# Sink values stacked four times in 32 rows, and the values products in another order

## The chip, the cores and the metric

The kernel runs on one core of a Trainium2 chip. Times are microseconds of device time of that core. The engines go by the names of the profile: PE is TensorE (PEld its weight loads), DVE is VectorE, ACT is ScalarE, POOL is GpSimd, and SP is SyncE, which here issues nearly all DMAs.

## The reference

Two stages. First attention over q, k, v of shape (4 batches, 8 heads, 768 positions, 64): a query sees the keys of its window (the last 128 positions) and the first `n_sink` = 4 positions of its batch, the sinks.

```
scores = q @ k.T / sqrt(64)
keep = (pos < n_sink) | ((rel >= 0) & (rel < window))
a = softmax(where(keep, scores, -1e9))
out = a @ v
```

Then a dense part on the result, its heads side by side, as x of shape 3072 x 512:

```
h = x @ w_in          # 512 -> 2048
g = h * cos(h)
result = g @ w_out    # 2048 -> 512
```

## The kernel before

A head's six blocks of 128 queries are taken two at a time, 256 queries. Per batch the first pair of blocks forms an early chunk, the other two pairs form late chunks; the 32 early heads and 64 late heads are each one head of one such chunk. Late heads are the ones that the change touches. For one, TensorE makes the scores of each block (`scores`, L1024, 264 columns: 128 keys of the block, 8 sink columns padded from 4, 128 keys before it), VectorE masks and reduces them (L1046), ScalarE takes the exponential (L1055), a scaling by the row's denominator follows (L1075 where it is on VectorE), and TensorE turns the probabilities (`turn`, L1136) so that keys stand in partitions. To keep the precision of fp32 on fast products, a number is split into a rounded high part and the rest, the low part. Of the turned probabilities ScalarE writes the high part (L1162), VectorE the low one (L1167), and GpSimd cuts each into the two triangles of the window (`split`, L1174), into the tile `ph`. In the same way `vr` holds v's high and low parts side by side, 2 x 64 columns.

The values product of a late head (`values`, L1196 to 1219) then adds seven matmuls into one PSUM tile `av` of 128 x 256. A product with 128 weight columns multiplies by both parts of v, into rows 0 to 63 and 64 to 127; one with 64 weight columns by the high part alone. Three key blocks take part: the middle one serves both query blocks (256 moving columns), the outer ones one each (128). The two halves of `av` are added afterwards (L1222, L1234).

The sinks come in by a product of their own. `load_batch_v` (L852) loads the sinks' rows of v of a batch into `yt`, 8 DMAs. `vs_part` (L1091), one step for each of four slots of 32 partitions, writes their high and low parts into `x1r`, two VectorE operations on 16 rows a step. Per four heads, `sink_cols` (L1101) copies the sink columns of the probabilities into `gc` as high and low columns, 4 heads x 32 columns; `sink_turn` turns them (L1120), and `sink_out` copies the result to `gt`. The sinks' product multiplies `gt` (moving) by `x1r` (weights).

The dense part is two products of 512 moving columns: `h` (L476) and `acc` (L521), each of three parts (high by high, high by low, low by high), with the cosine between them on ScalarE and VectorE (L485 to L512). A planner (`Plan.order`, L70) sets the program order of each engine ahead of time from costs and due times in a table `C`, and engines run their own lists strictly in that order. Buffers are few: a load or a product waits until the last user of its buffer is through. In the opening, 0 to 64 us, where early heads run and weights arrive, TensorE's list is filled with products that nothing reads (L1532).

Names in the order rows below: `av_1_2_0` is the PSUM tile of a late head, `ph` and `vr` its probabilities and values, `gt` the turned sinks, `x1r` the sinks' values, `acc` the dense output.

Of the kernel before, what the change touches and what calls it, by code (L numbers as in the profile page):

```python
# [9 lines left out]
F32 = mybir.dt.float32  # L10
# [6 lines left out]
P = 128  # L17
NSINK = 8
SW = P + NSINK
GR = 96 + 2 * NSINK  # L20
BW = 2 * P + NSINK
INV2PI = 1.0 / (2.0 * math.pi)
TWOPI_DOWN = 6.283185
# [149 lines left out]
def attn_moe_kernel(ctx, tc, q, k, v, n_sink, window, w_in, w_out, out):  # L173
# [51 lines left out]
    neg, quarter = neg3[:, 0:2], neg3[:, 2:3]  # L225
# [7 lines left out]
    def setup():  # L233

        nc.scalar.dma_start(out=nw_i[:, 0, :], in_=n_sink.unsqueeze(0))
        nc.scalar.dma_start(out=nw_i[:, 1, :], in_=window.unsqueeze(0))
        nc.gpsimd.memset(ident, 0.0)
        nc.gpsimd.affine_select(
            out=ident, in_=ident, pattern=[[-1, P]], compare_op=ALU.not_equal, fill=1.0, base=0, channel_multiplier=1
        )  # L240

        nc.gpsimd.iota(rc_i[:, 0], pattern=[[-1, P]], base=0, channel_multiplier=1)
        nc.gpsimd.iota(rc_i[:, 1], pattern=[[1, P]], base=0, channel_multiplier=0)
        nc.vector.memset(ones, 1.0)
        nc.vector.memset(quarter, HALF_PI_DOWN)
        for raw, src in env.first:
            nc.scalar.dma_start(out=raw.rearrange("p n w -> p (n w)"), in_=src)
        nc.scalar.activation(out=tiny[:, 0:1], in_=quarter, func=AF.Exp)
        nc.vector.memset(f32(one_r), 1.0)
        nc.vector.tensor_copy(out=one_r, in_=f32(one_r))  # L250
        nc.vector.memset(lims, 0.0)
        nc.vector.memset(lims[:, 0, 1, 0:1], 1.0)
        nc.vector.memset(lims[:, 1, 0, 0:1], float(NSINK))
        nc.vector.memset(lims[:, 1, 1, 0:1], float(P))
        nc.vector.tensor_single_scalar(out=minus, in_=ident, scalar=-1.0, op=ALU.mult)
        nc.vector.tensor_copy(out=rc, in_=rc_i)
        nc.vector.tensor_single_scalar(out=env.below, in_=rel, scalar=0.0, op=ALU.is_lt)

        with tc.tile_pool(name="warm", bufs=1, space=PSUM) as pool:
            warm = pool.tile([P, P], F32, name="warm")  # L260
            both = pool.tile([P, 2], F32, name="both")
            for _ in range(C["WARM"]):
                nc.tensor.matmul(out=warm, lhsT=ident, rhs=ident, start=True, stop=True)

            nc.vector.tensor_copy(out=nw4, in_=nw_i)
            nc.tensor.matmul(out=both, lhsT=ones, rhs=nw4[:, :, 0], start=True, stop=True)
            for _ in range(C["WARM2"]):
                nc.tensor.matmul(out=warm, lhsT=ident, rhs=ident, start=True, stop=True)
            nc.vector.tensor_copy(out=neg, in_=both)
# [526 lines left out]
    def banded_path(ctx2):  # L796
# [33 lines left out]
        def x1r():  # L830

            if env.x1r is None:
                env.x1r = ap.tile([P, NP * NT], F32R, name="x1r", tag="x1")
                env.vs = env.x1r.rearrange("p (a b c d) -> p a b c d", a=NP, b=2, c=2)
            return env.x1r

        def sink_values():
# [14 lines left out]
        def load_batch_v(o):  # L852
            def fn(e):
                o.vs32 = xb[:, : 2 * D].rearrange("p (n d) -> p n d", d=D)
                for h in range(4):
                    for dup in range(2):
                        r0 = h * 32 + dup * 8
                        nc.sync.dma_start(
                            out=o.vs32[r0 : r0 + 8], in_=v[o.b, h::4, 0:NSINK, :].rearrange("p s d -> s p d")
                        )  # L860
            return fn
# [228 lines left out]

        def vs_part(o, h):  # L1091
            def fn(e):
                w = sink_values().rearrange("p (g a) b c d -> p g (a b) c d", g=2)
                r = slice(h * 32, h * 32 + 2 * NSINK)
                e.tensor_copy(out=w[r, :, h, 0, :], in_=o.vs32[r])
                e.tensor_tensor(
                    out=w[r, :, h, 1, :], in0=o.vs32[r], in1=f32(w)[r, :, h, 0, :], op=ALU.subtract
                )
            return fn

        def sink_cols(o, four):  # L1101
            def fn(e):
                j0 = o.sj[0]
                for h, oo in enumerate(four):
                    nc.vector.tensor_copy(out=gc.bitcast(F32R)[:, j0:, h * 32 : h * 32 + NSINK], in_=oo.p[:, j0:, P:SW])
                for h, oo in enumerate(four):
                    nc.vector.tensor_tensor(
                        out=gc[:, j0:, h * 32 + NSINK : h * 32 + 2 * NSINK], in0=oo.p[:, j0:, P:SW],
                        in1=gc[:, j0:, h * 32 : h * 32 + NSINK], op=ALU.subtract,
                    )  # L1110
            return fn

# [2 lines left out]

        def sink_turn(o):
            def fn(e):
                o.gp = late_bank(o, 2)[:GR]
                for n, j in enumerate(o.sj):
                    nc.tensor.transpose(  # L1120
                        out=o.gp[:, n * P : (n + 1) * P], in_=gc[:, j], identity=ident,
                    )
            return fn

        def sink_out(o):
            def fn(e):
                w = len(o.sj) * P
                copy(e, gt[:GR, :w], o.gp[:, :w])
            return fn

        def turn(o):
# [64 lines left out]
        def values(o):  # L1196


            def fn(e):
                o.av = late_bank(o, 1)  # L1200
                mms = {}
                for t, w in ((o.phi, 2 * D), (o.plo, D)):
                    for n, (kb, qs) in enumerate(o.cols):
                        dst = o.av[:w, (qs[0] - o.i0) * P : (qs[-1] + 1 - o.i0) * P]
                        lhs = o.vr[:, kb - o.kb0].rearrange("p a d -> p (a d)")[:, :w]
                        mms.setdefault((w, len(qs)), []).append((dst, lhs, t[:, o.offs[n] * P : o.offs[n + 1] * P]))
                (wide_hi,), (wide_lo,) = mms[2 * D, CB], mms[D, CB]
                narrow = [m for pair in zip(mms[2 * D, 1], mms[D, 1]) for m in pair]
# [485 lines left out]
        gc = ap.tile([P, CB, GR], F32, name="gc")  # L1694
        env.x1f = ap.tile([P, NP, PT], F32, name="x1f", tag="x1")

        for _, _, fn, e in steps:
# [155 lines left out]
```

## Time and profile before

| what | value |
|---|---|
| median of 3 runs | 726.91 us (726.79 to 726.95) |
| span of the profiled execution | 725.6 us |
| PE busy | 708.8 us (98%) |
| PEld busy | 584.1 us (81%) |
| DVE busy | 599.3 us (83%) |
| ACT busy | 527.7 us (73%) |
| POOL busy | 127.5 us (18%) |

The profiled execution is listed by its span, from the first to the last instruction; a run's time also holds what lies around that. Busy times of PE overlap the engine's own pipelining, so a busy PE is not one at its peak. Four stages can be told apart: the opening to 64 us, early heads with dense products to 182, late heads with dense products to 620, dense products alone to the end. Within the third, batches begin near 185, 293, 405 and 517 us with the split of their sinks' values.

### The profile page before, as it was taken

The page shows a single profiled execution, that of the slowest core. Times are in us where ns is not written, and L with a number is a line of the kernel's source. Part 1 is how long each engine was busy: PE and PEld are TensorE (multiplying, and loading weights), DVE is VectorE, ACT ScalarE, POOL GpSimd, SP SyncE. Part 2 cuts the span into 40 slices and gives each one's busy share as a digit, 9 for nine tenths or more (in the row PEclk, how much of TensorE's full clock was granted, in tenths as well). Part 3 has the DMA queues.
Part 4 walks back from the last instruction along what each step waited for, and adds up shares of the span by engine and source line. Part 5 has one row for each costly group of instructions (what it writes and reads, how often), then busy time and mean ns, then how long its engine had stood idle before and what let it go on. Part 6 is the DMA issues. An engine that isn't in the chain of part 4 may idle for free.

```text
span 725.6 us, 12986 instructions
## 1 busy us (share of the span) xinstructions
PE 708.8 (98%) x3674; PEld 584.1 (81%) x3674; DVE 599.3 (83%) x1849; ACT 527.7 (73%) x1344; POOL 127.5 (18%) x213
## 2 busy tenths in 40 slices
PE   7998999999999999999999999999999999999996
PEld 7766787888888888888888888888888888888884
DVE  6889998988988978988978988878989865667762
ACT  3896976788697697796686886776887766566642
POOL 1010000001223222232231222232123222100000
PEclk9999999999999999999999999999999999999999
DMA  5665555533256333355433254433254500375551
GB/s 144 182 186 153 158 162 162 141 65 68 68 118 146 73 62 57 72 119 124 93 60 59 56 131 103 118 61 64 43 139 99 119 18 12 97 210 148 164 137 64
DMA packets 236501, 77.13 MB, mean 106 GB/s; under 512 B 221060, under 2 KB 221060, under 8 KB 236420
## 3 DMA queue, kind: packets, MB, share of 16 engines
q1 hardware_dynamic: 236128, 75.15, 43.4%
q10 hardware_dynamic: 292, 1.05, 0.5%
q8 instruction: 32, 0.52, 0.3%
q14 instruction: 49, 0.40, 0.2%
HBM read 69.86 MB, written 6.29 MB: 105 GB/s over the span
## 4 chain that ended last, share of the span: by engine, by line
PE 81%; ACT 11%; DVE 4%; issue 2%; DMA 1%; SPq 0%; ACTq 0%; DVEq 0%
PE acc L521 32%; PE h L476 32%; PE av L1215 5%; PE s L1024 4%; ACT p L1055 3%; PE s L968 2%; PE av L1191 2%; PE tp L1136 2%; ACT p L1073 1%; PE tp L1146 1%; PE qk L931 1%; ACT L485 1%; PE idle L1532 1%; ACT L1055 1%; ACT early L390 1%
## 5 line engine op out<-in xcount | busy, mean ns | idle before, releaser
L521 PE MATMUL acc<-whi_out,ghi 128*128 128x512 f32 x384 | 161.8, 421 | 0.0
L476 PE MATMUL h<-xhi,whi_in 128*128 128x512 f32 x384 | 155.2, 404 | 0.0
L476 PE MATMUL h<-xlo,whi_in 128*128 128x512 f32 x384 | 150.9, 393 | 0.0
L521 PE MATMUL acc<-whi_out,glo 128*128 128x512 f32 x384 | 150.8, 393 | 0.0
L521 PE MATMUL acc<-wlo_out,ghi 128*128 128x512 f32 x384 | 150.1, 391 | 0.0
L476 PE MATMUL h<-xhi,wlo_in 128*128 128x512 f32 x384 | 150.0, 391 | 0.0
L1174 POOL TENSOR_SCALAR_AFFINE_SELECT ph<-ph 128x512 fp32r<-128x512 f32 x128 | 87.4, 683 | 230.3 <-DVE ph L1167 226.4
L485 ACT ACTIVATE r<-h 128x512 f32<-128x512 f32 x96 | 57.1, 598 | 48.6 <-PE h L476 46.0
L476 PEld LDWEIGHTS h<-xlo,whi_in 128*128 128x128 f32 x384 | 72.1, 188 | 16.3
L521 PEld LDWEIGHTS acc<-whi_out,glo 128*128 128x128 f32 x384 | 72.1, 188 | 16.2
L476 PEld LDWEIGHTS h<-xhi,whi_in 128*128 128x128 f32 x384 | 72.2, 188 | 12.0 <-DVE r L498 0.3
L476 PEld LDWEIGHTS h<-xhi,wlo_in 128*128 128x128 f32 x384 | 72.4, 189 | 11.2
L521 PEld LDWEIGHTS acc<-whi_out,ghi 128*128 128x128 f32 x384 | 72.8, 190 | 10.7
L521 PEld LDWEIGHTS acc<-wlo_out,ghi 128*128 128x128 f32 x384 | 72.7, 189 | 9.4
L1055 ACT ACTIVATE p<-p,st 128x136 f32<-128x136 f32 (+1 forms) x192 | 79.2, 416 | 0.3
L498 DVE SCALAR_TENSOR_TENSOR r<-r,h 128x512 f32<-128x512 f32 x96 | 64.6, 674 | 16.9 <-ACT r L491 16.1
L506 ACT CAST ghi<-r 128x512 fp32r<-128x512 f32 x96 | 59.5, 619 | 22.8 <-PE acc L521 15.7
L512 DVE TENSOR_TENSOR glo<-r,ghi 128x512 fp32r<-128x512 f32 x96 | 66.3, 691 | 7.1 <-ACT ghi L506 6.3
L1046 DVE CUSTOM_DVE_ANT_0 p<-s,mk 128x136 f32<-128x136 f32 (+1 forms) x192 | 59.8, 313 | 6.5 <-PE s L968 3.1
L984 ACT CAST l<-tq 64x256 fp32r<-64x256 f32 x64 | 25.8, 403 | 46.7 <-PE s L1024 46.4
L1032 DVE COPY_PREDICATED s<-mk,s 128x128 f32<-128x128 int32 x128 | 37.3, 291 | 24.6 <-PE s L1024 22.5
L1024 PEld LDWEIGHTS s<-r,l 128*128 128x128 f32 x256 | 46.5, 188 | 12.3 <-DVE ph L1167 1.5
(153 smaller groups left out, 1302.3 us busy)
## 6 DMA issues: line engine op xcount, KB each, us to landing
xk<-in_k_dram SPq DMA_DIRECT2D x256, 48.0 KB
raw<-in_moe_w_out_dram SPq DMA_DIRECT2D x16, 512.0 KB
wt<-in_moe_w_in_dram SPq DMA_DIRECT2D x32, 256.0 KB
raw<-in_moe_w_in_dram SPq DMA_DIRECT2D x14, 512.0 KB
v<-in_v_dram SPq DMA_DIRECT2D x64, 96.0 KB
raw<-in_v_dram SPq DMA_DIRECT2D x32, 192.0 KB
out_dram<-wt SPq DMA_DIRECT2D x22, 256.0 KB
wt<-in_moe_w_out_dram SPq DMA_DIRECT2D x20, 256.0 KB
```

The costliest lines, as they stand in the source:

```text
L476: nc.tensor.matmul(out=o.h, lhsT=w[:, c, fs], rhs=xx[:, c, :], start=(c == 0 and n == 0), stop=(c == NC - 1 and n == 2),)
L485: nc.scalar.activation(out=o.r, in_=o.h, func=AF.Sin, scale=0.5)
L498: nc.vector.scalar_tensor_tensor(out=o.r, in0=o.r, scalar=0.5, in1=o.h, op0=ALU.subtract, op1=ALU.mult)
L506: nc.scalar.copy(out=o.ghi, in_=o.r)
L512: e.tensor_tensor(out=o.glo, in0=o.r, in1=f32(o.ghi), op=ALU.subtract)
L521: nc.tensor.matmul(out=y.acc[j], lhsT=gg[:, j * P : (j + 1) * P], rhs=w[:, f, :], start=(f == 0 and n == 0), stop=(f == NFT - 1 and n == 2),)
L1024: nc.tensor.matmul(out=o.s_ps[j][:, :w], lhsT=o.l[:, j * P : (j + 1) * P], rhs=r.rearrange("p n s -> p (n s)")[:, c0 : c0 + w], start=(n = ...
L1032: nc.vector.copy_predicated(out=o.s_ps[j][:, :P], mask=below.bitcast(I32), data=o.s_ps[j][:, SW : SW + P])
L1046: nc.vector.tensor_tensor_reduce(out=o.pj[j][:, :w], in0=o.s_ps[j][:, :w], in1=masks[min(o.i0 + j, 2)][:, :w], op0=ALU.add, op1=ALU.min, s ...
L1055: nc.scalar.activation(out=o.pj[j][:, :w], in_=o.pj[j][:, :w], func=AF.Exp, bias=o.lead.st[:, 0, o.nth, j : j + 1], scale=-1.0, accum_out= ...
L1174: nc.gpsimd.affine_select(out=ph[:, :, b, :], in_=f32(ph)[:, :, 1, :], pattern=[[0, 2 * CB], [(-1, 1)[b], P]], compare_op=(ALU.is_gt, ALU. ...
L1215: nc.tensor.matmul(out=dst, lhsT=lhs, rhs=rhs, start=(n == 0), stop=(n == len(seq) - 1), skip_group_check=True)
```

## The change

It has three parts. In `values` the seven products are issued in another order: both parts of the first key block, the sinks, both parts of the last key block, the middle block's low part, and the middle block's high part with 256 moving columns at the end. The sinks' product takes 64 weight columns in place of 128, and `x1r` is laid out for that: in each slot of 32 rows the 8 sink rows stand four times, as high, high, low, low. For that `load_batch_v` loads each row group four times (16 DMAs a batch, not 8), and `vs_part` has three operations on 32 rows: round, multiply by a per-partition number `odd16` (0 or -1, by partition), add the loaded values. The columns of `gc` become high, low, high, low of each head, so `sink_cols` writes twice the elements; the transposes of `gc` and the copy to `gt` cover 128 columns and partitions in place of 112. The setup gains one iota on GpSimd and two VectorE operations for `odd16`.

```diff
@@ setup
+        nc.gpsimd.iota(odd16.bitcast(I32), pattern=[[0, 1]], base=0, channel_multiplier=1)
...
+        nc.vector.tensor_scalar(
+            out=odd16.bitcast(I32), in0=odd16.bitcast(I32), scalar1=4, scalar2=1,
+            op0=ALU.logical_shift_right, op1=ALU.bitwise_and,
+        )
+        nc.vector.tensor_single_scalar(out=odd16, in_=odd16.bitcast(I32), scalar=-1.0, op=ALU.mult)
@@ load_batch_v
-                    for dup in range(2):
+                    for dup in range(4):
                         r0 = h * 32 + dup * 8
@@ vs_part
-                r = slice(h * 32, h * 32 + 2 * NSINK)
-                e.tensor_copy(out=w[r, :, h, 0, :], in_=o.vs32[r])
-                e.tensor_tensor(
-                    out=w[r, :, h, 1, :], in0=o.vs32[r], in1=f32(w)[r, :, h, 0, :], op=ALU.subtract
-                )
+                r = slice(h * 32, h * 32 + 32)
+                w = sink_values()[r, :, h // 2, h % 2, :]
+                e.tensor_copy(out=w, in_=o.vs32[r])
+                e.tensor_scalar(out=w, in0=f32(w), scalar1=odd16[r], scalar2=1.0, op0=ALU.mult, op1=ALU.mult)
+                e.tensor_tensor(out=w, in0=f32(w), in1=o.vs32[r], op=ALU.add)
@@ sink_cols
-                    nc.vector.tensor_copy(out=gc.bitcast(F32R)[:, j0:, h * 32 : h * 32 + NSINK], in_=oo.p[:, j0:, P:SW])
+                    nc.vector.tensor_copy(
+                        out=g5.bitcast(F32R)[:, :, h, :, 0],
+                        in_=oo.p[:, :, P:SW].unsqueeze(2).broadcast_to([P, CB, 2, NSINK]),
+                    )
...
-                        out=gc[:, j0:, h * 32 + NSINK : h * 32 + 2 * NSINK], in0=oo.p[:, j0:, P:SW],
-                        in1=gc[:, j0:, h * 32 : h * 32 + NSINK], op=ALU.subtract,
+                        out=g5[:, :, h, :, 1], in0=oo.p[:, :, P:SW].unsqueeze(2).broadcast_to([P, CB, 2, NSINK]),
+                        in1=g5[:, :, h, :, 0], op=ALU.subtract,
@@ values
-                seq = [wide_hi]
-                if o.sj:
-                    lhs = sink_values()[:, o.pair, o.odd].rearrange("p a d -> p (a d)")
-                    seq.append((o.av[:, o.sj[0] * P :], lhs, gt[:, : len(o.sj) * P]))
-                seq += [*narrow[:2], wide_lo, *narrow[2:]]
+                sinks = o.av[:D], sink_values()[:, o.h // 4, o.pair % 2, o.odd], gt
+                seq = [
+                    block(0, o.phi, 2 * D), block(0, o.plo, D), sinks, block(2, o.phi, 2 * D),
+                    block(2, o.plo, D), block(1, o.plo, D), block(1, o.phi, 2 * D),
+                ]
```

The planner's costs for these steps are as they were, so the lists of the engines keep their steps in the same order; what moves stands inside the steps.

TensorE, the values group of the first head of batch 1 and the dense product behind it, before (weight rows or columns are not in the row; its shape is that of the result):

```order
L1215 MATMUL av_1_2_0_3657<-ph_1_2_0_3588,vr_1_2_0_3524 128x256
L1215 MATMUL av_1_2_0_3657<-gt_78,x1r_2138 128x256
L1215 MATMUL av_1_2_0_3657<-ph_1_2_0_3588,vr_1_2_0_3524 128x128
L1215 MATMUL av_1_2_0_3657<-ph_1_2_0_3588,vr_1_2_0_3524 64x128
L1215 MATMUL av_1_2_0_3657<-ph_1_2_0_3588,vr_1_2_0_3524 64x256
L1215 MATMUL av_1_2_0_3657<-ph_1_2_0_3588,vr_1_2_0_3524 128x128
L1215 MATMUL av_1_2_0_3657<-ph_1_2_0_3588,vr_1_2_0_3524 64x128
L521 MATMUL acc_16_0_2335<-whi_out_91,ghi_31_3566 128x512
```

The same place after the change:

```order
L1219 MATMUL av_1_2_0_3684<-ph_1_2_0_3611,vr_1_2_0_3539 128x128
L1219 MATMUL av_1_2_0_3684<-ph_1_2_0_3611,vr_1_2_0_3539 64x128
L1219 MATMUL av_1_2_0_3684<-gt_78,x1r_2149 64x256
L1219 MATMUL av_1_2_0_3684<-ph_1_2_0_3611,vr_1_2_0_3539 128x128
L1219 MATMUL av_1_2_0_3684<-ph_1_2_0_3611,vr_1_2_0_3539 64x128
L1219 MATMUL av_1_2_0_3684<-ph_1_2_0_3611,vr_1_2_0_3539 64x256
L1219 MATMUL av_1_2_0_3684<-ph_1_2_0_3611,vr_1_2_0_3539 128x256
L526 MATMUL acc_16_0_2350<-whi_out_91,ghi_31_3589 128x512
```

The group's last product had 128 moving columns and now has 256; the sinks' product (`gt`) is third and not second, and writes 64 rows of `av`.

VectorE at the start of batch 1, before (`x1r` is the sinks' values, `yt` what was loaded):

```order
L512 TENSOR_TENSOR glo_3608<-r_3461,ghi_3566 128x512
L1095 CAST x1r<-yt 16x2x64
L1096 TENSOR_TENSOR x1r<-yt,x1r 16x2x64
L1032 COPY_PREDICATED s_2_5_0_3615<-mk,s_2_5_0_3615 128x128
L392 CAST gt<-gp_2_0_3618 112x256
```

The same place after the change:

```order
L517 TENSOR_TENSOR glo_3631<-r_3476,ghi_3589 128x512
L1100 CAST x1r<-yt 32x2x64
L1101 TENSOR_SCALAR x1r<-x1r,neg 32x2x64
L1102 TENSOR_TENSOR x1r<-x1r,yt 32x2x64
L1037 COPY_PREDICATED s_2_5_0_3638<-mk,s_2_5_0_3638 128x128
L397 CAST gt<-gp_2_0_3641 128x256
```

One operation more stands in the step; three more such steps follow a little later in the same list, and nothing else has moved.

SyncE's queue in the opening, before:

```order
L568 DMA raw_70<-in_moe_w_in_dram 128x1024
L858 DMA yt<-in_v_dram 8x2x64 x8
L923 DMA xq<-in_q_dram 128x2x64 x2
L923 DMA xk<-in_k_dram 128x2x64 x2
L568 DMA raw_71<-in_moe_w_in_dram 128x1024
```

The same place after the change:

```order
L573 DMA raw_70<-in_moe_w_in_dram 128x1024
L863 DMA yt<-in_v_dram 8x2x64 x16
L928 DMA xq<-in_q_dram 128x2x64 x2
L928 DMA xk<-in_k_dram 128x2x64 x2
L573 DMA raw_71<-in_moe_w_in_dram 128x1024
```

Eight more loads stand ahead of the next head pair's q and k.

## Rows read from the trace of the kernel before

**Rows 1.** Stages: us; busy us (count) of PE, PEld, DVE, ACT, POOL; PEclk
```profile
182.00:620.00 438.00, 436.82 (x2344) 363.56 (x2343) 373.89 (x1220) 334.81 (x870) 117.80 (x187) 1.00 0.39 83
```

**Rows 2.** Chain of waits, 182 to 620 us, shares of the stretch by line
```profile
by line: PE h L476 34.3%; PE acc L521 33.1%; PE av L1215 7.4%; PE s L1024 5.8%; PE tp L1136 3.2%; ACT p L1055 2.9%; issue 2.1%; ACT p L1073 1.8%; ACT L485 1.2%; ACT L1055 1.0%; ACT r L1009 0.8%; ACT vr L1083 0.8%; PE gp L1120 0.7%; ACT yt L
```

**Rows 3.** Table by stretch, at the start of batches 0 and 1
```profile
185.00:198.00 13.00, 13.00 (x71) 10.92 (x70) 12.00 (x35) 8.50 (x20) 3.05 (x5) 1.00 0.27 70
293.00:304.00 11.00, 11.00 (x57) 8.89 (x56) 10.68 (x41) 9.05 (x20) 1.86 (x3) 1.00 0.26 51
```

**Rows 4.** Costliest groups: weight loads of acc (busy us, mean ns | idle)
```profile
L521 PEld LDWEIGHTS acc<-whi_out,ghi 128*128 128x128 f32 x384 | 72.8, 190 | 10.7
```

**Rows 5.** Timeline of TensorE: start us, us, line; behind values, behind a score pair
```profile
401.59 0.52 PE L1215 MATMUL av<-ph,vr 128*128 128x128 f32 x5
401.94 0.45 PE L521 MATMUL acc<-whi_out,ghi 128*128 128x512 f32 x1
402.23 0.39 PE L521 MATMUL acc<-wlo_out,ghi 128*128 128x512 f32 x1
402.45 0.40 PE L521 MATMUL acc<-whi_out,glo 128*128 128x512 f32 x1
...
411.41 0.40 PE L521 MATMUL acc<-whi_out,ghi 128*128 128x512 f32 x1
411.64 0.40 PE L521 MATMUL acc<-wlo_out,ghi 128*128 128x512 f32 x1
```

**Rows 6.** Timeline of VectorE, the split of the sinks' values, batch 0
```profile
185.58 0.21 DVE L1095 CAST x1r<-yt 16x128 fp32r<-16x128 f32 x1
185.83 0.28 DVE L1096 TENSOR_TENSOR x1r<-yt,x1r 16x128 fp32r<-16x128 f32 x1
186.14 0.22 DVE L1095 CAST x1r<-yt 16x128 fp32r<-16x128 f32 x1
```

**Rows 7.** Groups by shape, VectorE (busy us, mean ns | idle)
```profile
L1075 DVE TENSOR_SCALAR p<-p,st 128x136 f32<-128x136 f32 x43 | 9.5, 285 | 0.0
L1105 DVE CAST gc<-p 128x16 fp32r<-128x16 f32 x64 | 7.4, 174 | 1.9 <-ACT p L1073 1.9
L1107 DVE TENSOR_TENSOR gc<-p,gc 128x16 f32<-128x16 f32 x64 | 6.8, 168 | 0.0
```

**Rows 8.** Timelines of VectorE, then TensorE, batch 1
```profile
297.28 0.73 DVE L1096 TENSOR_TENSOR x1r<-yt,x1r 16x128 fp32r<-16x128 f32 x1
302.00 0.68 DVE L498 SCALAR_TENSOR_TENSOR r<-r,h 128x512 f32<-128x512 f32 x1
303.69 0.38 DVE L1167 TENSOR_TENSOR ph<-tp,ph 128x256 fp32r<-128x256 f32 x1
...
302.90 0.40 PE L476 MATMUL h<-xhi,whi_in 128*128 128x512 f32 x1
304.27 0.40 PE L1024 MATMUL s<-r,l 128*128 128x264 f32 x2
```

**Rows 9.** Timelines of SyncE's issues (opening, batch 2), then TensorE in the opening
```profile
10.27 3.74 SPq L858 DMA_DIRECT2D yt<-in_v_dram  x8
14.53 0.91 SPq L923 DMA_DIRECT2D xq<-in_q_dram  x2
20.43 1.68 SPq L923 DMA_DIRECT2D xk<-in_k_dram  x2
...
404.04 2.67 SPq L858 DMA_DIRECT2D yt<-in_v_dram  x8
...
18.54 0.38 PE L931 MATMUL qk<-ident,xq 128*128 128x128 f32 x2
24.54 0.38 PE L931 MATMUL qk<-ident,xk 128*128 128x128 f32 x2
```

**Rows 10.** Timeline: a small load's issue, and the operation that waited for it
```profile
1.38 0.22 ACTq L236 DMA_DIRECT2D nw_i<-in_window_dram  x1
2.96 0.16 DVE L265 CAST sm<-nw_i 1x4 f32<-1x4 int32 x1 [0.19 <-DMA nw_i<-in_window_dram]
```

More of the change, by code (lines that the diff above doesn't have):

```diff
@@ L19 @@
 SW = P + NSINK
-GR = 96 + 2 * NSINK
 BW = 2 * P + NSINK
@@ L224, in attn_moe_kernel @@
     neg3 = cp.tile([P, 4], F32, name="neg")
-    neg, quarter = neg3[:, 0:2], neg3[:, 2:3]
+    neg, quarter, odd16 = neg3[:, 0:2], neg3[:, 2:3], neg3[:, 3:4]
     lims = cp.tile([1, 2, 2, 2], F32, name="lims")
@@ L833, in x1r @@
                 env.x1r = ap.tile([P, NP * NT], F32R, name="x1r", tag="x1")
-                env.vs = env.x1r.rearrange("p (a b c d) -> p a b c d", a=NP, b=2, c=2)
+                env.vs = env.x1r[:, : NP * 2 * D].rearrange("p (g a o d) -> p g a o d", g=2, o=2, d=D)
             return env.x1r
@@ L1092, in fn @@
             def fn(e):
-                w = sink_values().rearrange("p (g a) b c d -> p g (a b) c d", g=2)
-                r = slice(h * 32, h * 32 + 2 * NSINK)
-                e.tensor_copy(out=w[r, :, h, 0, :], in_=o.vs32[r])
-                e.tensor_tensor(
-                    out=w[r, :, h, 1, :], in0=o.vs32[r], in1=f32(w)[r, :, h, 0, :], op=ALU.subtract
-                )
+                r = slice(h * 32, h * 32 + 32)
[3 more added lines that the diff above has]
+                e.tensor_tensor(out=w, in0=f32(w), in1=o.vs32[r], op=ALU.add)
             return fn
@@ L1102, in fn @@
             def fn(e):
-                j0 = o.sj[0]
+                g5 = gc.rearrange("p j (h r c s) -> p j h r c s", r=2, c=2, s=NSINK)
                 for h, oo in enumerate(four):
-                    nc.vector.tensor_copy(out=gc.bitcast(F32R)[:, j0:, h * 32 : h * 32 + NSINK], in_=oo.p[:, j0:, P:SW])
+                    nc.vector.tensor_copy(
+                        out=g5.bitcast(F32R)[:, :, h, :, 0],
+                        in_=oo.p[:, :, P:SW].unsqueeze(2).broadcast_to([P, CB, 2, NSINK]),
+                    )
                 for h, oo in enumerate(four):
                     nc.vector.tensor_tensor(
-                        out=gc[:, j0:, h * 32 + NSINK : h * 32 + 2 * NSINK], in0=oo.p[:, j0:, P:SW],
-                        in1=gc[:, j0:, h * 32 : h * 32 + NSINK], op=ALU.subtract,
+                        out=g5[:, :, h, :, 1], in0=oo.p[:, :, P:SW].unsqueeze(2).broadcast_to([P, CB, 2, NSINK]),
+                        in1=g5[:, :, h, :, 0], op=ALU.subtract,
                     )
@@ L1117, in fn @@
             def fn(e):
[L1118 to L1122, printed above, removed]
+                o.gp = late_bank(o, 2)
+                for j in range(CB):
+                    nc.tensor.transpose(out=o.gp[:, j * P : (j + 1) * P], in_=gc[:, j], identity=ident)
             return fn
@@ L1126, in fn @@
             def fn(e):
-                w = len(o.sj) * P
-                copy(e, gt[:GR, :w], o.gp[:, :w])
+                copy(e, gt, o.gp)
             return fn
@@ L1200, in fn, with block @@
                 o.av = late_bank(o, 1)
[L1201 to L1208, printed above, removed]
-                seq = [wide_hi]
-                if o.sj:
-                    lhs = sink_values()[:, o.pair, o.odd].rearrange("p a d -> p (a d)")
-                    seq.append((o.av[:, o.sj[0] * P :], lhs, gt[:, : len(o.sj) * P]))
-                seq += [*narrow[:2], wide_lo, *narrow[2:]]
+                def block(n, t, w):
+                    kb, qs = o.cols[n]
+                    return (
+                        o.av[:w, (qs[0] - o.i0) * P : (qs[-1] + 1 - o.i0) * P],
+                        o.vr[:, n].rearrange("p a d -> p (a d)")[:, :w], t[:, o.offs[n] * P : o.offs[n + 1] * P],
+                    )
+                sinks = o.av[:D], sink_values()[:, o.h // 4, o.pair % 2, o.odd], gt
[3 more added lines that the diff above has]
+                ]
                 for n, (dst, lhs, rhs) in enumerate(seq):
@@ L1693, in banded_path @@
         ps = env.ps = ctx2.enter_context(tc.tile_pool(name="ps", bufs=1, space=PSUM))
-        gc = ap.tile([P, CB, GR], F32, name="gc")
+        gc = ap.tile([P, CB, P], F32, name="gc")
         env.x1f = ap.tile([P, NP, PT], F32, name="x1f", tag="x1")
```

## The prediction

> **What bounds the kernel now.** I read the table by stages first. In the stage of the late heads, 182 to 620 us, TensorE is busy for 436.82 of 438.00 us at a granted clock of 1.00 [rows 1]: an edit there pays what it changes on TensorE, or what it makes TensorE wait for. Then the chain of waits over the same stage: PE h 34.3%, acc 33.1%, av 7.4%, s 5.8%, tp 3.2%, gp 0.7%, together 84.5%; the rest is ScalarE, VectorE and issue [rows 2]. So about 0.85 of a saving on TensorE shows in the end, and an addition on VectorE shows where TensorE is waiting for it. Where that is, the busy time of short stretches says: after the start of batch 1 VectorE is busy 10.68 of 11.00 us, while TensorE is busy for all of them; at the start of batch 0 VectorE has more air, 12.00 of 13.00 us [rows 3].
>
> **The values products (gain).** Each of the 64 late heads issues seven products. Before, the last has 128 moving columns, and the dense product behind it needs a load of 128 weight columns, 190 ns by its row [rows 4]. In the timeline that dense product starts at 401.94, the next at 402.23, the one after at 402.45: steps of 0.29 and 0.22 us. Where a dense group follows the two score products of 264 columns, its first step is 411.41 to 411.64, 0.23 us [rows 5]. So 0.29 - 0.23 = 0.06 us is lost once per head behind the short product; the five last products together take 0.35 us (401.59 to 401.94), so the load has no long product to hide behind. I take 0.055, between the two neighbouring steps. After the change a product of 256 columns comes last, and every load of 128 weight columns stands behind a longer one; the group's moving columns are the same three times 256 and four times 128, so its own length stays. At most 64 x 0.055 = 3.5 us. Some three heads behind each of the four batch starts run at VectorE's pace (below), which leaves 52, and of these 0.85 counts: 52 x 0.055 x 0.85 = 2.4 us. Bounds: 0 and 3.5. The narrower load of the sinks' product (64 columns for 128) is hidden either way, behind a product of 128 columns or more.
>
> A rule speaks against this term. The Trainium skill, "TensorE: Matmul & The Clock Gate", section "Architectural detail: the array is 16× 32×32, not 1× 128×128", says that a matmul can begin before its weight load has completed. The rows agree that the dense product starts soon after the short one; but its successor starts late, so the time is paid one product later. Taken by itself the rule would make this term 0.
>
> **The split of the sinks' values (loss).** Per batch four steps had two operations each and now have three, on 32 partitions of 128 elements in place of 16; 16 operations are added. VectorE's time goes by elements in a partition, so the old two keep theirs. The rows in batch 0 show how such a chain steps: a cast at 185.58, its subtraction at 185.83 (0.25 later, 0.21 busy), the next cast at 186.14 (0.31 later, 0.28 busy) [rows 6]; a dependent operation costs its duration and 0.03. The added one takes its scalar from a pointer, like the one that takes 285 ns for 136 elements [rows 7]: 0.285 + 0.03 = 0.315, four times 1.26 us a batch. From below a cast's step, 4 x 0.25 = 1.0. From above, one of the four takes the 0.73 that a subtraction took beside GpSimd's work [rows 8]: 1.26 + 0.45 = 1.7.
>
> What lies over it: the chain runs on through VectorE's queue, in program order. Behind the four steps in batch 1 come the cosine's operation at 302.00 (0.68 us), whose end frees the bank for TensorE's h product at 302.90, about 0.2 us later, and the low part at 303.69 (0.38 us), ended at 304.07, before the score product at 304.27 [rows 8]. So TensorE's cover is 0.2 us, and VectorE has no idle time to give back in between. 1.26 - 0.2 = 1.1 us on TensorE in each of batches 1, 2 and 3, which look alike. In batch 0 VectorE's air is spread over the same stretch (1.0 us, some 0.5 of it before TensorE next needs it), so 0.7. Sum 3 x 1.1 + 0.7 = 4.0 us. Bounds: 3 x 0.8 + 0.2 = 2.6 from the cheaper step, 3 x 1.5 + 1.2 = 5.7 from the dearer. TensorE has next to nothing to catch up with afterwards [rows 1].
>
> **The sinks' columns (small loss).** 16 groups of eight operations now write 32 elements a partition in place of 16. A cast grows from 174 ns at 16 elements to some 220 at 128 [rows 6, 7], 0.41 ns an element, so 7 ns; a subtraction from 168 to 284, 1.04 ns, so 17 ns. 64 x 7 + 64 x 17 = 1.5 us on VectorE. Three of the 16 groups stand in the busy stretches, others just ahead of what TensorE waits for; I count 0.5, bounds 0 and 1.5. The transposes load 128 columns in place of 112: behind dense products, nothing to 0.2.
>
> **The loads (loss in the opening, nothing later).** SyncE issues eight loads of the sinks' values at 10.27 in 3.74 us, then at 14.53 the next head pair's q [rows 9]. Eight more take at least the 2.67 us of a later batch; the queue would come to q at about 14.01 + 2.67 + 0.1 = 16.8, 2.2 us late, and at 3.74 us 3.3 late. TensorE takes that q in at 18.54, 3.58 us after the second of its two issues (14.53 + 0.91/2). How much of that is landing? The next k, two issues from 20.43 to 22.11, the second begun about 21.65 (an issue takes half of 0.91), is worked on at 24.54, so a landing takes no more than some 2.9 [rows 9]; a load of a few bytes issued at 1.38 was waited for until 2.96, so no less than 1.6 [rows 10]. Cover 0.7 to 2.0: TensorE is late by 0.2 to 1.5, with the slower issue 2.6. I take 1.0, a landing near 2.4, since q is larger than the small load and may share its engines with weights. In that stretch the chain of waits runs through TensorE, so it stays in the end. In batches 1 to 3 the added loads delay the next k by about 2.7 us; VectorE, itself 1.26 late there, covers that, and I count nothing; if not, 0.5 a batch.
>
> **The setup.** One GpSimd and two tiny VectorE operations stand before VectorE's 1.35 us wait for TensorE. Nothing.
>
> **Sum.** 1.0 + 4.0 + 0.5 - 2.4 = +3.1 us. The profiled execution's span is 725.6 us, the median of the runs 726.91, so 1.3 us lie around the span: 725.6 + 3.1 + 1.3 = 730.0 us.
>
> **Rivals.** (A) Faster: VectorE's added work is swallowed. It holds if TensorE's next needs of VectorE lie over 1.26 us away behind each batch start; then 1.0 + 0.2 for the opening and columns, and 64 x 0.055 = 3.5 with nearly all heads, less 0.3: -2.0, so 724.9. For it: VectorE is idle for 64 us of the stage [rows 1]. Against it: the 0.2 us at 302.90 and 304.27. It decides from the point where the cover exceeds 1.26 us. (B) No change: the added operation costs a cast's step, 1.0 a batch, and the cover is 0.4 (4 x 0.6 = 2.4 in place of 4.0), the opening hides 0.6 of its 1.0, and the reorder gives 3.0: 0.4 + 2.4 + 0.4 - 3.0 = +0.2, so 727.1. For it: bounds that reach so far. Against it: four sizes would all have to err one way. (C) Slower still: the reorder gives nothing, because the hitch moves into the group (a load behind one of the short products that now come first) or a late load is not what makes the step of 0.29: 1.0 + 4.0 + 0.5 = 5.5, so 732.4. The rule named above would end there too. For it: short products now stand in a row at the group's head. Against it: the 0.23 steps at 411.41. (D) The opening loses 2.6 in place of 1.0, with the rest as forecast: 731.6.
>
> **How the numbers follow.** The forecast (with D beside it) gets 0.54, C 0.15, B 0.17, A 0.14. What a measurement can tell here is about 0.2%, 1.45 us. A gives faster; B, with a little of the forecast's lower end, the same; the rest slower: faster 0.14, same 0.20, slower 0.66. The range runs from 726.2, which leaves out A, to 733.0, which takes in C and the dearer steps but not all together; the forecast's own range is 728.5 to 731.8.
>
> **What would show it.** The first dense step behind a values group should read 0.23 and not 0.29. The split should read three operations, the middle one near 0.28 us, and all four steps should take 3.5 us in batch 0 where they take 2.2 (185.58 to 187.8). At each batch start TensorE should show a wait of about 1 us within 5 to 10 us, in its h or score products, ended by VectorE. The row of sixteen loads should end near 16.7, and the q transposes at 18.54 be near 19.5. If VectorE's added time leaves no gaps on TensorE, the forecast is wrong by A; if the dense step stays at 0.29, by C.

## The result and the profile after

The change makes the kernel slower: 732.8 us in the median of 5 runs (731.32 to 734.4) beside 726.91 for before (726.7 to 726.95), a ratio of 1.008 (95% interval 1.0069 to 1.0092). A second series, with other runs of before, gave 1.0073 (1.0059 to 1.0086). The forecast was 730.0, slower by 3.1 us; measured are 5.9. The direction held. The result lies above the forecast's own range (728.5 to 731.8) and 0.2 us inside the wider one (up to 733.0): the order gave back much less than forecast, and the loads cost more.

The page of the profiled execution, its span and its engines:

```profile
span 730.6 us, 13063 instructions
PE 709.1 (97%) x3674; PEld 579.3 (79%) x3674; DVE 605.2 (83%) x1867; ACT 529.2 (72%) x1344; POOL 128.0 (18%) x214
```

and the table by stage, where TensorE is busy for 433.56 of 438 us and was for 436.82 [rows 1]:

```profile
182.00:620.00 438.00, 433.56 (x2321) 355.37 (x2321) 376.81 (x1235) 333.76 (x864) 117.11 (x188) 1.00 0.38 84
```

So TensorE now waits in a stage in which it hardly did. The step that the order was to remove is gone. The timeline of TensorE round a values group of batch 2 (start us, us, line):

```profile
404.13 0.41 PE L1029 MATMUL s<-r,l 128*128 128x264 f32 x2
404.37 0.28 PE L1219 MATMUL av<-ph,vr 128*128 128x128 f32 x2
404.49 0.28 PE L1219 MATMUL av<-gt,x1r 128*64 128x256 f32 x1
404.62 0.51 PE L1219 MATMUL av<-ph,vr 128*128 128x128 f32 x4
404.97 0.39 PE L526 MATMUL acc<-whi_out,ghi 128*128 128x512 f32 x1
405.20 0.40 PE L526 MATMUL acc<-wlo_out,ghi 128*128 128x512 f32 x1
```

The first dense product behind the group steps in 0.23 us (404.97 to 405.20), where it took 0.29 [rows 5]; the group itself still takes 0.60.

The split of the sinks' values, VectorE in batch 1, the first slot and the second:

```profile
298.71 0.21 DVE L1100 CAST x1r<-yt 32x128 fp32r<-32x128 f32 x1
298.95 0.54 DVE L1101 TENSOR_SCALAR x1r<-x1r,neg 32x128 fp32r<-32x128 f32 x1
299.53 0.73 DVE L1102 TENSOR_TENSOR x1r<-x1r,yt 32x128 fp32r<-32x128 f32 x1
301.04 0.22 DVE L1100 CAST x1r<-yt 32x128 fp32r<-32x128 f32 x1
301.29 0.28 DVE L1101 TENSOR_SCALAR x1r<-x1r,neg 32x128 fp32r<-32x128 f32 x1
301.60 0.28 DVE L1102 TENSOR_TENSOR x1r<-x1r,yt 32x128 fp32r<-32x128 f32 x1
301.91 0.22 DVE L1100 CAST x1r<-yt 32x128 fp32r<-32x128 f32 x1
```

The middle operation takes 0.28 us and steps in 0.31, as forecast from [rows 6, 7]; beside GpSimd's work (298.27 to 300.12) two operations of the first slot are longer, the last of them by as much as in before [rows 8]. In batch 0 the four steps run from 186.84 until VectorE's next operation at 190.32, 3.48 us. Behind them TensorE waits, a little earlier in its list than at the two places of [rows 8]: at the transposes of the probabilities.

```profile
303.91 0.40 PE L526 MATMUL acc<-whi_out,glo 128*128 128x512 f32 x1
304.93 0.41 PE L1140 MATMUL tp<-ident,p 128*128 128x128 f32 x2 [0.62 <-DVE st L1051]
305.10 0.47 PE L526 MATMUL acc<-whi_out,ghi 128*128 128x512 f32 x1
```

The waits of TensorE in the stage, from its table of waits (us in total, times, longest), where before has a single row of 0.8 us, for the transposes:

```profile
PE tp L1140 <- DVE st L1051: 2.6, 7, 0.6
PE tp L1140 <- ACT p L1078: 0.7, 3, 0.3
PE acc L526 <- DVE glo L517: 0.5, 1, 0.5
PE gp L1127 <- DVE gc L1114: 0.2, 1, 0.2
```

In the opening, SyncE's sixteen loads and the q behind them, which [rows 9] show at 10.27 and 14.53:

```profile
9.78 6.75 SPq L863 DMA_DIRECT2D yt<-in_v_dram  x16
16.63 0.91 SPq L928 DMA_DIRECT2D xq<-in_q_dram  x2
```

and TensorE, which took that q in at 18.54 without a wait and now waits 2.00 us for it:

```profile
19.09 0.41 PE L936 MATMUL qk<-ident,xq 128*128 128x128 f32 x2 [2.00 <-DMA xq<-in_q_dram]
```

The sinks' columns, by shape, have grown by 7 and 19 ns [rows 7]:

```profile
L1109 DVE CAST gc<-p 128x32 fp32r<-128x32 f32 x64 | 7.9, 181 | 1.7 <-ACT p L1078 1.7
L1114 DVE TENSOR_TENSOR gc<-p,gc 128x32 f32<-128x32 f32 x64 | 7.9, 187 | 0.0
```

**Where the time goes.** TensorE's list has the same order in both kernels, so each of its matmuls can be found in both timelines. The table gives how much later each stands than its counterpart in before, as differences of starts (us), worked out for the kernels below: the opening and the early heads (to 180), the four batch starts (188 to 198, 289 to 306, 403 to 420, 515 to 532 by before's times), the four stretches between and behind these (198 to 289, 306 to 403, 420 to 515, 532 to 619), and the rest. One profiled execution each, so the first column carries its scatter.

| kernel | to 180 | four batch starts | between | rest | end |
|---|---|---|---|---|---|
| after | +1.2 | +0.83 +1.16 +1.18 +1.20 | -0.59 | +0.28 | +5.26 |
| after_again | +1.5 | +0.84 +1.21 +1.21 +1.20 | -0.85 | +0.25 | +5.39 |
| e1_order | -0.2 | 0.0 +0.02 +0.08 +0.04 | +0.38 | 0.0 | +0.35 |
| e2_two_ops | +2.3 | -0.08 +0.68 +0.37 +0.48 | -0.68 | +0.25 | +3.31 |
| e3_loads | +0.1 | +0.85 +1.17 +1.18 +1.22 | -0.62 | +0.24 | +4.14 |
| e4_cols | +2.0 | +0.84 +1.08 +1.09 +1.11 | -1.03 | +0.27 | +5.35 |
| e5_three | -0.1 | -0.08 -0.03 -0.02 -0.02 | -1.12 | +0.20 | -1.21 |
| e8_nosinks | -0.1 | -0.14 +0.06 +0.07 +0.06 | -2.46 | +0.47 | -2.05 |
| e6_slots | +2.2 | -0.08 +1.77 +1.35 +1.23 | -0.86 | +0.24 | +5.87 |
| e7_pool | +0.8 | -0.07 +1.72 +1.61 +1.35 | -0.66 | +0.23 | +5.01 |
| e9_fused | +2.7 | -0.08 +0.46 +0.16 +0.27 | -0.68 | +0.27 | +3.13 |
| e11_spread | -0.8 | -0.04 -0.02 -0.02 -0.01 | -0.67 | +0.25 | -1.32 |
| e13_extra | -1.2 | +0.11 +0.08 +0.03 +0.07 | +1.84 | +0.95 | +1.86 |

Before itself stands at 0 by definition, and its profiled opening is one draw too: six other kernels with eight loads at that place stand at -1.2 to +0.1. With them and before the mean is -0.33; the six with sixteen loads on SyncE stand at +1.2 to +2.7, mean 1.99. So the opening costs 2.3 us by the traces (1.4 to 1.9 by the runs of e3_loads beside those of after), the batch starts cost 4.4, and 0.6 comes back between them. Those 0.6 are the order's gain less what the doubled sink columns take in these stretches: the eight kernels with doubled columns stand at -0.59 to -0.86 there, the two with the new order and single ones (e4_cols, e5_three) at -1.03 and -1.12.

### The profile page after: what moved, and what is told of

Same layout as the page of the kernel before. It is cut to its first block, busy times and chain, and to the rows that moved or that the text cites. A ratio compares the mean times of both kernels' runs of the same rounds, so it can differ in the third digit from the quotient of the medians.

```text
span 730.6 us, 13063 instructions
## 1 busy us (share of the span) xinstructions
PE 709.1 (97%) x3674; PEld 579.3 (79%) x3674; DVE 605.2 (83%) x1867; ACT 529.2 (72%) x1344; POOL 128.0 (18%) x214
## 4 chain that ended last, share of the span: by engine, by line
PE 69%; ACT 13%; DVE 10%; issue 4%; DMA 3%; SPq 1%; ACTq 0%; DVEq 0%
PE h L481 27%; PE acc L526 26%; ACT p L1060 4%; PE s L1029 3%; PE av L1219 3%; PE av L1195 2%; PE s L973 2%; PE tp L1140 2%; ACT p L1078 1%; ACT L1060 1%; DMA raw<-in_moe_w_in_dram 1%; PE tp L1150 1%; DVE glo L517 1%; ACT L490 1%; DMA xq<-in_q_dram 1%
## 5 line engine op out<-in xcount | busy, mean ns | idle before, releaser
L526 PE MATMUL acc<-whi_out,ghi 128*128 128x512 f32 x384 | 160.0, 417 | 0.0
```

The costliest lines, as they stand in the source:

```text
L526: nc.tensor.matmul(out=y.acc[j], lhsT=gg[:, j * P : (j + 1) * P], rhs=w[:, f, :], start=(f == 0 and n == 0), stop=(f == NFT - 1 and n == 2),)
```

## The experiments

Theory A before them: the loss is the third operation (batch starts) and the sixteen loads (opening), and the order gains on TensorE. The rivals are in the expectations. Each ratio is to runs of before in the same series.

**e1_order: the order alone.**

```diff
-                seq = [wide_hi]
-                ...
-                seq += [*narrow[:2], wide_lo, *narrow[2:]]
+                seq = [*narrow[:2], sinks, *narrow[2:], wide_lo, wide_hi]
```

> The kernel before with the new order of the seven values products alone; the sinks' product keeps 128 weight columns. Theory A (a load of 128 weight columns behind a product of 128 moving columns costs 0.054 us, wherever it stands): the order now puts the sinks' load behind a short product, so the step of 0.28 at the first dense product falls to 0.23 and the sinks' product, or the one behind it, grows by 0.05: 726.9 us, within 0.5. Rival B (only the dense product behind a short one pays): 64 x 0.053 = 3.4 us less on TensorE, 723.5 to 724.5.

Measured: 727.7 us (727.25 to 728.14), ratio 1.0004 (0.9995 to 1.0012). TensorE, the group and the dense products behind it:

```profile
401.40 0.28 PE L1213 MATMUL av<-ph,vr 128*128 128x128 f32 x2
401.52 0.33 PE L1213 MATMUL av<-gt,x1r 128*128 128x256 f32 x1
401.69 0.52 PE L1213 MATMUL av<-ph,vr 128*128 128x128 f32 x4
402.05 0.40 PE L521 MATMUL acc<-whi_out,ghi 128*128 128x512 f32 x1
402.29 0.39 PE L521 MATMUL acc<-wlo_out,ghi 128*128 128x512 f32 x1
```

The dense step is 0.24 (402.05 to 402.29), and the sinks' product now takes 0.17 (401.52 to 401.69) where it took 0.12. The 0.05 us has moved to the next place where a load of 128 columns stands behind a short product. The 64 columns are thus a condition of the order's gain, not an ornament.

**e2_two_ops: no third operation.**

```diff
-                e.tensor_scalar(out=w, in0=f32(w), scalar1=odd16[r], scalar2=1.0, op0=ALU.mult, op1=ALU.mult)
```

> The kernel after, without the multiplication in the split of the sinks' values (two operations a step; the low rows then hold something else). Theory A (the third operation holds VectorE for 1.26 us a batch and TensorE waits for it): the waits of 0.6 to 0.8 us at 189.7, 302.0, 414.1 and 526.3 go, 3.3 to 4.2 us less than the kernel after, 728.6 to 729.5. Rival B (the eight more loads of a batch make the next k late and that is what TensorE feels): 732.5, the waits stay.

Measured: 730.38 (729.21 to 730.65), ratio 1.0034 (1.0022 to 1.0047): about 0.45% less than after, 3 us, a little under the 3.3 to 4.2 expected. The batch starts fall from 4.4 to 1.45. What is left there is the rival in a smaller size. VectorE in batch 1, in front of the transposition of the next k:

```profile
304.73 0.34 DVE L1093 TENSOR_TENSOR vr<-v,vr 128x192 fp32r<-128x192 f32 x1
305.99 0.58 DVE L1002 STREAM_TRANSPOSE tk<-xk 128x384 f32<-128x384 f32 x1 [0.92 <-DMA xk<-in_k_dram]
```

The k that stands behind sixteen loads on SyncE is 0.92 us late for VectorE. In after VectorE came so late itself that this could not be seen.

**e3_loads: eight loads a batch.**

```diff
-                    for dup in range(4):
+                    for dup in range(2):
```

> The kernel after with the sinks' values loaded into the first 16 of each 32 rows only, eight loads a batch as before (the other 16 rows hold what stood there). Theory A (the loads cost in the opening alone): the wait of 2.0 us for q near 17 us goes, 1.2 to 1.9 less than the kernel after, 731.0 to 731.6, the waits at the batch starts stay, and the runs lie closer together than the 731.3 to 734.4 of the kernel after. Rival B (they cost at the batch starts): 4 us less, 728.8.

Measured: 731.01 (730.82 to 733.55), ratio 1.0054 (1.004 to 1.0067). SyncE's loads and the q behind them, near the times of before:

```profile
10.32 3.84 SPq L863 DMA_DIRECT2D yt<-in_v_dram  x8
14.26 0.91 SPq L928 DMA_DIRECT2D xq<-in_q_dram  x2
```

The opening's loss is gone (+0.1), the batch starts are those of after to 0.03 us. The spread of the runs did not shrink clearly.

**e4_cols: the sinks' columns once.**

```diff
-                        in_=oo.p[:, :, P:SW].unsqueeze(2).broadcast_to([P, CB, 2, NSINK]),
+                nc.vector.tensor_copy(out=g5.bitcast(F32R)[:, :, h, 0, 0], in_=oo.p[:, :, P:SW])
```

> The kernel after with the sinks' columns copied once, not twice (16 elements a partition as before; the second half of the columns stays zero). Theory A (the longer columns make the transposes of the sinks wait, 0.2 us at 9 of 16 groups, and this is where part of the gain of the order goes): 0.8 to 1.5 less than the kernel after, 731.3 to 732.0. Rival B (the wait only moves to the next product that the slower engines hold up): 732.8, no change.

Measured: 732.9 (732.73 to 734.25), ratio 1.0078 (1.0065 to 1.0091): no change that these runs can tell, but their intervals leave room for 1 us either way. In its one trace the batch starts are 0.25 and the stretches between 0.4 better than in after; the opening drew 0.8 worse, which hides it in the sum. The 0.4 has a place: at the four transposes of the sink columns that TensorE meets between the batch starts, the step into them is 0.20 us longer than in before in after and 0.09 here. So the traces put the doubled columns at some 0.6 us, which the runs neither show nor exclude.

**e5_three: all three additions off; what is left is the order with 64 columns.** The edits of e2_two_ops, e3_loads and e4_cols together.

> The kernel after with all three additions taken off at once: two operations a step in the split, eight loads a batch, the sinks' columns copied once (the low parts of the sinks' values and the second half of the columns are left out). What stays is the new order with 64 weight columns. Theory A (TensorE sets the pace between the batch starts, so the 0.053 us a head comes through): 2.4 to 3.0 less than the kernel before, ratio 0.996. Theory B (there TensorE and the softmax chain on ScalarE and VectorE are level, and what TensorE saves it waits for at the next transposes): 0.8 to 1.4 less, ratio 0.998 to 0.999. In both the waits at the batch starts and the wait for k at about 306 are gone.

Measured: 725.93 (724.95 to 727.65), ratio 0.9985 (0.9976 to 0.9993), theory B: 1.1 us. The batch starts are at 0. By the differences of their steps, the dense products behind the values groups save 3.3 us over the stage; a third of it arrives. In the stretches between the batch starts 2.9 us are saved and 1.8 come back as longer steps elsewhere in TensorE's list, about half of them at its transposes. TensorE's waits in the stage:

```profile
PE tp L1135 <- DVE st L1051: 1.1, 4, 0.3
PE tp L1135 <- ACT p L1078: 0.7, 3, 0.2
```

Before had 0.8 us in the first of these rows and none of the second.

**e8_nosinks: does TensorE set the pace?**

```diff
-                if o.sj:
+                if False:
                     lhs = sink_values()[:, o.pair, o.odd].rearrange("p a d -> p (a d)")
                     seq.append((o.av[:, o.sj[0] * P :], lhs, gt[:, : len(o.sj) * P]))
```

> The kernel before without the sinks' product in the values group, six products in place of seven (that part of the result is left out); all else stays. TensorE has 0.117 us less to do in each of 64 heads, 7.5 us. Theory A (TensorE sets the pace in the stage of the late heads): about 0.85 of it, 6 us less, 721. Theory B (the softmax chain is level with it): 1 to 3 us less, 724 to 726, and TensorE's busy share in the stage falls, with waits at the transposes.

Measured: 724.54 (724.06 to 726.26), ratio 0.9965 (0.9952 to 0.9979): 2.5 of 7.5 us. The stage, and TensorE's waits in it:

```profile
182.00:620.00 438.00, 434.75 (x2293) 356.52 (x2292) 375.44 (x1222) 336.72 (x875) 118.08 (x187) 1.00 0.39 84
```

```profile
PE tp L1136 <- DVE st L1046: 1.3, 4, 0.3
PE tp L1136 <- ACT p L1073: 0.8, 3, 0.3
PE gp L1120 <- DVE gc L1107: 0.5, 3, 0.2
PE tp L1136 <- DVE p L1075: 0.5, 3, 0.2
```

TensorE's busy time fell from 436.82 to 434.75, and it waits 3.1 us for probabilities and sink columns, where it waited 0.8. Step by step, 6.3 us are saved between the batch starts and 3.9 come back: 2.5 at the transposes, 1.0 at score products, the rest in small steps elsewhere.

**e13_extra: the other direction.**

```diff
-                seq += [*narrow[:2], wide_lo, *narrow[2:]]
+                seq += [*narrow[:2], narrow[1], wide_lo, *narrow[2:]]
```

> The kernel before with one of the seven values products of each late head issued twice (64 weight columns, 128 moving columns; that term is counted twice in the result): TensorE has 0.059 us more in each of 64 heads, 3.8 us. If TensorE and the softmax chain are level between the batch starts, adding costs in full, 3 to 3.8 us, ratio 1.004 to 1.005, though taking twice as much away gave 2.6 of 7.5. If the softmax chain were ahead of TensorE as the bound, adding would cost under 1.5.

Measured: 729.66 (728.93 to 730.16), ratio 1.0036 (1.0023 to 1.005): 2.6 of 3.8 us, 0.7 of what was added, and in the trace 3.1 (the end less the opening). Of the 3.1, 0.8 is a single wait at a product near 651 us, 30 us behind the last late head (e8_nosinks lost 0.6 at the same product); without it 2.3 remain, 0.6 of what was added. The ratio lies just under what was expected of level chains; its interval, 1.7 to 3.6 us, leaves out the 1.5 of a softmax chain ahead of TensorE, but by little. The stage:

```profile
182.00:620.00 438.00, 437.44 (x2395) 366.72 (x2394) 371.90 (x1212) 333.08 (x868) 116.01 (x187) 1.00 0.38 83
```

Adding costs 0.6 to 0.7 of itself, taking away gives a third.

**e6_slots and e7_pool: another layout with fewer operations.**

```diff
+                if h == 0:
+                    e.tensor_copy(out=x.bitcast(F32R), in_=o.vs32)
+                    e.tensor_tensor(out=x[64:].bitcast(F32R), in0=o.vs32[64:], in1=x[64:], op=ALU.subtract)
+                e.tensor_scalar(
+                    out=sink_values()[:, :, h // 2, h % 2, :], in0=x, scalar1=slot[:, h : h + 1], scalar2=1.0,
+                    op0=ALU.mult, op1=ALU.mult,
+                )
```

> The same product with 64 weight columns, its parts laid out another way: high rows in partitions 0 to 63, low rows in 64 to 127, so one rounding and one subtraction a batch serve all four slots, and four independent multiplications by a 0/1 mask per slot write the weights (6 operations a batch; 8 before, 12 after). Sixteen loads a batch as in the kernel after. VectorE at a batch start: 0.25 + 0.31 + 4 x 0.20 = 1.4 us, 0.9 less than before. Theory A (VectorE's own time made the batch starts late, the loads the opening): opening +1.6 to +2.2, batch starts 0 to +0.5 each from the late k, the order -0.6: 728 to 730. Rival (the longer waits come from the wider partitions or the layout): as the kernel after, 732.8.

> The kernel of e6_slots with half of the sixteen loads issued by GpSimd, so SyncE issues eight as before. Theory A (the price of the loads is SyncE's queue ahead of q and k): the opening's wait and the late k go, 1.5 to 3 us less than e6_slots, 726 to 727.5. Rival (the transfers themselves or GpSimd's issuing cost as much): as e6_slots or slower.

Measured: e6_slots 733.8 (732.93 to 735.65), ratio 1.0093 (1.0078 to 1.0108); e7_pool 732.43 (731.3 to 733.49), ratio 1.007 (1.0056 to 1.0083). Both expectations failed (728 to 730, and 726 to 727.5). VectorE, the four masks in batch 0 and the first operation in batch 1:

```profile
188.45 0.88 DVE L1099 TENSOR_SCALAR x1r<-yt,neg 128x128 fp32r<-128x128 f32 x4
...
300.98 0.23 DVE L1097 CAST yt<-yt 128x128 fp32r<-128x128 f32 x1 [2.18 <-DMA yt<-in_v_dram]
```

The operations are as cheap as expected (batch 0 costs nothing, -0.08), but the first of them reads all four slots, so it needs all sixteen loads, and VectorE's whole queue stands 2.18 us behind it. In after the first step needs its own slot's four loads. In e7_pool the opening improves by 1.4 us in the trace, while the same operation still waits 2.11 us for a DMA.

**after_again, e9_fused, e11_spread: one operation for two, and the loads out of the way.**

```diff
-                e.tensor_scalar(out=w, in0=f32(w), scalar1=odd16[r], scalar2=1.0, op0=ALU.mult, op1=ALU.mult)
-                e.tensor_tensor(out=w, in0=f32(w), in1=o.vs32[r], op=ALU.add)
+                e.scalar_tensor_tensor(
+                    out=w, in0=f32(w), scalar=odd16[r], in1=o.vs32[r], op0=ALU.mult, op1=ALU.add
+                )
```

and for e11_spread, in `load_batch_v` and `load_v`:

```diff
+                        if dup % 2 and o.b == 0:
+                            later.append(load)
+                        else:
+                            load(nc.gpsimd if dup % 2 else nc.sync)
...
+                if later and o.early and o.a >= 2:
+                    later.pop(0)(nc.sync)
```

> The kernel after once more, beside the three that follow, so that they are compared within one series: 731.5 to 734 us, ratio 1.007 to 1.009.

> The kernel after with the multiplication and the addition of the split fused into one operation (w * odd16 + v with the per-partition scalar), two operations a step as before the change, the result whole. Theory A (it is the third operation's time on VectorE): 2.0 to 3.0 less than the kernel after, and what is left at the batch starts is the wait of 0.9 us for k behind sixteen loads, 0.4 to 0.7 on TensorE each. Rival (32 partitions or the pointer make the pair as dear as three): as the kernel after.

> e9_fused with the eight more loads taken out of SyncE's way: in batch 0 they are spread over eight later heads, in the other batches GpSimd issues them. Theory A (opening: q behind sixteen loads; later batches: k behind them): opening within 0.3 of the kernel before, batch starts 0 to 0.4 late each, the order -0.6 over the stretches between: 726.5 to 727.5, the same as the kernel before. Rival (the additions on VectorE still cost): 728 to 729.

Measured: after_again 732.82 (731.73 to 733.0), 1.0073; e9_fused 729.59 (729.08 to 730.45), 1.0034 (1.0022 to 1.0046); e11_spread 726.38 (725.66 to 727.42), 0.9994 (0.9985 to 1.0003). Fusing is worth 3.2 us. VectorE in e9_fused, the second slot:

```profile
301.04 0.22 DVE L1100 CAST x1r<-yt 32x128 fp32r<-32x128 f32 x1
301.29 0.34 DVE L1101 SCALAR_TENSOR_TENSOR x1r<-x1r,neg,yt 32x128 fp32r<-32x128 f32 x1
301.66 0.22 DVE L1100 CAST x1r<-yt 32x128 fp32r<-32x128 f32 x1
```

The fused operation takes 0.34. In e11_spread GpSimd and SyncE issue eight loads each, beside one another:

```profile
291.24 4.72 POOL L867 DMA_DIRECT2D yt<-in_v_dram  x8 [0.30 <-DVE raw L1250]
```

```profile
290.95 2.67 SPq L867 DMA_DIRECT2D yt<-in_v_dram  x8
```

All four batch starts are at 0 (-0.09 together), and so is the opening, within its scatter. Beside e9_fused the runs are 3.2 us shorter, as much as the table gives for the loads: 2.3 in the opening and 0.9 at the batch starts. e11_spread keeps all that after computes, without the costs in the opening and at the batch starts; its 0.6 us under before are within the interval.

## Why the prediction was right or wrong

**Split of the sinks' values: right.** Forecast 4.0; measured 4.4 to 4.5 at the batch starts, of which some 0.3 go with the columns (e4_cols: 4.1). e2_two_ops takes 2.9 of it away, e9_fused 3.6; what is left in e2_two_ops goes with the late k, which takes over, and is gone in e11_spread. The duration (0.28) and the step (0.31) were as forecast. The place was not: the first wait is at the transposes (304.93) or an `acc` product, not at `h`.

**Columns: about right, but by traces alone.** 0.5 was forecast, bounds 0 and 1.5; the traces give some 0.6, 0.3 at the batch starts and 0.3 to 0.4 between them. The runs of e4_cols can't tell it from nothing.

**Loads in the opening: right mechanism, too small.** Forecast 1.0, bounds 0.2 to 2.6; measured 2.3 in the mean. The queue came to q nearly when computed (16.63 for 16.8), in part by luck: the eight more loads took 3.0 us (6.75 less 3.74) where 2.67 was taken as the least, and the row began 0.49 us earlier. The first wait follows the computed way: the q product stands at 19.09 in place of 18.54, 0.55 late, with a landing of 2.0 us where 2.4 was taken. (The 3.58 us that the prediction reads between issue and product is 3.56 by its own numbers; nothing hangs on it.) What the sum left out is what follows behind this first wait: two things that the last section here shows. For the later batches the forecast counted nothing and 0.5 a batch if the cover were gone; e2_two_ops shows 0.4 to 0.7 of it as soon as VectorE's delay is taken off.

**Order: the step that failed.** Forecast -2.4; measured -0.6 together with the columns, some -1.1 by itself. "Some three heads behind each of the four batch starts run at VectorE's pace (below), which leaves 52, and of these 0.85 counts: 52 x 0.055 x 0.85 = 2.4 us." The 0.055 held (0.052 to 0.053 in every group), the 0.85 did not. TensorE's share of the chain of waits was read as a price for a saved microsecond. Between the batch starts the softmax chain on ScalarE and VectorE runs about level with TensorE, and much of what TensorE saves it waits for again, above all at its transposes: of 3.3 us saved behind the values groups 0.6 came through in after and 1.1 in e5_three, and 2.5 of 7.5 in e8_nosinks, while added work cost 0.6 to 0.7 of itself in e13_extra.

**The sum.** With the measured terms, 2.3 for the opening, 4.4 at the batch starts, 0.6 given back between them and 0.2 lost after the stage (in each kernel with the new sinks; that was not pursued) make 6.3, beside 5.9 in the runs. Forecast were 1.0 + 4.5 - 2.4. The gap of 2.8 is thus about 1.3 from the opening and, with split and columns near their forecasts, the rest from the order. The 1.3 us outside the span joined a span and a median of different runs: a run of before in a later series has 726.65 with a span of 724.9, 1.75 outside, and after 732.33 with 730.6. Before's profiled execution was thus some 0.4 us above its median, which agrees with the mean of -0.33 above.

**Rivals.** A (VectorE's work swallowed) is refuted by the waits at all four batch starts. B (no change) needed a cheaper operation and more cover: the operation stepped in 0.31, and 0.8 to 1.2 us came through at each batch start. C's number (732.4) was nearest, for another reason: the hitch did go, and it was the time that did not come. By the Trainium skill, "TensorE: Matmul & The Clock Gate", section "Architectural detail: the array is 16× 32×32, not 1× 128×128", a matmul can begin before its load completes; the runs show the hitch all the same, 0.05 us in before and in e1_order, gone in after, so here the measurement decides against reading that rule as a free load. D (2.6 in the opening, 731.6) had the opening nearly right and the order wrong.

## What to carry to other kernels

A share of the chain of waits is no price: where two chains run about level, as here, a saved microsecond was worth a third and an added one about two thirds of itself, so test it by taking a whole piece of work away before an edit is priced. Look for the burst in which an engine is full (here VectorE for 10 us after each batch start): there four added operations of 0.31 us cost the whole kernel 1.1 to 1.2 of their 1.24 us in three of the four batches, and fusing two operations into one was worth 3.2 us, more than the better order elsewhere (1.1). A queue of small loads is paid by whatever stands behind it, and the price of a late load is not only its wait.

## What the runs showed of the hardware

**The clock after a wait.** In after TensorE was idle for 2.00 us before 19.09. The granted clock, third from the end in each row of the table by stretch, was still 1.00 from 19 to 20 us; from 21 to 23 us it was half (1.2 of 2.4 GHz), though TensorE was busy throughout, and from 24 us on it was 1.00 again:

```profile
20.00:21.00 1.00, 1.00 (x8) 0.89 (x7) 0.41 (x2) 0.28 (x2) 0.00 (x0) 0.77 0.79 262
21.00:22.00 1.00, 1.00 (x7) 1.00 (x5) 0.85 (x3) 1.00 (x4) 0.00 (x0) 0.50 0.94 289
22.00:23.00 1.00, 1.00 (x5) 0.94 (x5) 0.80 (x2) 1.00 (x5) 0.00 (x0) 0.50 0.92 232
23.00:24.00 1.00, 1.00 (x5) 0.78 (x4) 0.94 (x4) 0.52 (x4) 0.00 (x0) 0.53 0.96 300
```

after_again (wait 2.08) and e2_two_ops (2.37) show the same; e4_cols, e6_slots and e9_fused, with waits of 0.73 to 1.15 at that place, stay at 1.00, and so does e9_fused behind a wait of 1.86 us at 26.00. That the wait brought the clock down is argued from these six traces; no run changes the wait alone. The waits differ in part because TensorE came to that q at different times: in the three kernels with the lower clock it was 1.4 to 1.6 us ahead of before in its list, in the other three 0.1 to 0.7. In after the lateness of 0.55 us at 19.09 was 0.67 at the k product behind it (20.22), with the clock still at 1.00, and 1.59 by 24: four score products that took 0.92 us take 1.54. The clock's price was in no row of before, where TensorE is never idle for so long in this stretch.

**A load behind others.** In e9_fused the clock stayed, and the opening was the worst of all (+2.7). Its chain of waits shows two landings of q (start us, us):

```profile
17.29 1.97 DMA xq<-in_q_dram
...
20.25 5.62 DMA xq<-in_q_dram
```

The first took 1.97 us, the next pair's 5.62 (in e6_slots 4.46, and in e4_cols the k behind it 5.14). Its q was issued 0.91 us behind a weight load (18.88 and 19.79), where in before 2.4 us lay between the two (16.55 and 18.95). That the weights' transfer held it is argued from this order, not shown by a run.
